# First batch of a spectral filter: the order in which a second transpose writes, and one 128-column matmul per point of the last transform

## The chip, the cores and the metric

The kernel runs on one core of a Trainium2 chip. The metric is the device time of one launch in microseconds; a time quoted for the kernel is the median of several runs. One further execution was recorded by the hardware profiler. Its engines are called PE (TensorE), PEld (the weight loads of TensorE), DVE (VectorE), ACT (ScalarE), POOL (GpSimd) and SP (SyncE, which issues DMAs). All times below are microseconds unless ns is written.

## What is computed

```python
def _attn_ref(x, filt_r, filt_i):                 # x: 8 x 3008 x 256
    X = np.fft.rfft(x, axis=1)
    F = (filt_r + 1j * filt_i)[None, :, :]
    y = np.fft.irfft(X * F, n=x.shape[1], axis=1)
    return y.astype(np.float32)

def _moe_ref(x, w_in, w_out):                     # 24064 tokens, 256 -> 2048 -> 256
    h = x @ w_in
    g = np.maximum(0.01 * h, h)
    return g @ w_out

reference(...) = _moe_ref(_attn_ref(x, filt_r, filt_i).reshape(24064, 256), moe_w_in, moe_w_out)
```

Each of 8 batches is filtered along its 3008 positions in the frequency domain; then every token goes through two matrix products with a leaky ReLU between them.

## The kernel before

**Transforms as matmuls.** 3008 is 94 x 32, written n = 32 n1 + n2. The filter is done in four matmul steps. Step 1 transforms over n1 with the constant `fwd1`. Step 2 transforms over the 32 values of n2 (with the twiddle factors in the constant `f2_sb`), and the result is multiplied by the filter. Step 3, called `sa` in the names, transforms back to n2 (`inv2r`, `inv2i`). Step 4, called `sb`, transforms back to n1 (constant `i1_sb`, one 128 x 94 matrix for each n2) and gives `yt`, the filtered batch with the feature d on the partitions: `yt[:, dt]` holds the features of half dt, 128 partitions by 3008 positions. Between steps 1 and 2, and between 3 and 4, the data has to be turned. In batches 1 to 7 that goes through a scratch array in DRAM. In the first batch, where nothing else can run yet, VectorE turns it with a 32 x 32 block transpose of 4-byte words; each word is a pair of neighbouring 2-byte values (d even, d odd).

**The first batch by hand.** `FIRST` (L461) is a list of steps in the order in which they are issued; each engine takes its own steps in that order. `sap` (L417) is step 3 for four values; `sae` (L422) evacuates it from PSUM to `big[2]`. The helper `paired` (L278) views a tile as (e n t): for each e (one of 64 word columns in a half) and each of 32 n, two neighbouring values t. `t2 i` (L426) transposes a quarter of `big[2]` into `big[0]`, 128 x 1024 words; quarters 0 and 1 belong to half dt = 0, quarters 2 and 3 to dt = 1. `sbp dt h b` (L440) does step 4 for half dt and the four n2 of group h, into the PSUM bank b; the data of `big[0]` is the stationary operand (the weights) and `i1_sb[:, n2, :]` is streamed. `sbe` (L443) evacuates the 128 x 376 result into `yt`, on ScalarE (A) or VectorE (D), through `quad_copy` (L333). In the list stand all eight groups of dt = 0 and the groups 0 and 1 of dt = 1. The transposes are issued in the order 1, 0, 3, 2, after VectorE's last multiplies by the filter (`s2d`, L402).

**The rest is planned.** After the list, the MoE runs over 47 chunks of 512 tokens, 8 planner time units a chunk (`SL`). All later work is a heap of (time, function) pairs; what has the earliest planned time is issued first. The first MoE product (`moe1`, L499) needs `yt` for both halves; L509 is its matmul, L514 its evacuation with the leaky ReLU. The second product is L634 in the first three chunks and L573 later. The transforms of the next batches (L254, L303, L325, L346) are planned between these matmuls. The groups 2 to 7 of step 4 for dt = 1 of the first batch are planned there too: `late_sb` (L446), six calls at the times in `REST`, among the first nine chunks' matmuls. They call the same `sb_matmuls` (L431) as `sbp`. Step 4 of the later batches is `sb_group` (L338): one matmul (L346) for each n2 with 128 columns of weights and 96 rows.

**Layout of `big[0]` before.** Written by `t2` as (h n e r): for each half h, each pair of n2 (n), each of 64 e, the two n2 of the pair (r) side by side. One partition's word for e and n2 has, as its neighbour, the word for the same e and the other n2 of the pair. Since a word holds two values t, `sb_matmuls` reads, for one n2, the values of one t at every fourth 2-byte place: 64 columns for t = 0 and 64 for t = 1, in two matmuls that write the PSUM partitions 0 to 63 and 64 to 127. `sae` puts the features 0 to 63 of a half into t = 0 and 64 to 127 into t = 1, so that the two results are in the order of d.

Of the kernel before, what the change touches and what calls it, by code (L numbers as in the profile page):

```python
# [13 lines left out]
FP32 = mybir.dt.float32  # L14
# [7 lines left out]
Q = 32  # L22
# [53 lines left out]
def kernel(  # L76
# [9 lines left out]
    nc = tc.nc  # L86
# [42 lines left out]
    i1_sb = cpool.tile([P, N2, N1], FP16, name="i1_sb")  # L129
# [7 lines left out]
    big = [cpool.tile([P, Q * D], FP16, name=f"big{i}") for i in range(3)]  # L137
# [140 lines left out]
    def paired(t):  # L278
        return t[:].rearrange("p (e n t) -> p n e t", n=Q, t=2)
# [79 lines left out]
    held, spare = {}, [scrp.tile([P, 4, DH], FP32, tag=f"p{i // 2 + 1}", name=f"spare{i}") for i in range(6)]  # L359
# [61 lines left out]

    def sae(hf, c, e):  # L422
        engine[e](paired(big[2])[:, ds(c, 4), ts(hf, DH // 2)],
                  held.pop(("sa", hf, c)).rearrange("p n (t e) -> p n e t", t=2))

    def t2(i):  # L426
        a = big[2][:].bitcast(FP32)[:, ts(i, E4 * Q)].rearrange("p (e n r) -> p e n r", n=Q // 2, r=2)
        o = big[0][:].bitcast(FP32).rearrange("p (h n e r) -> p h e n r", h=2, n=Q // 2, r=2)
        nc.vector.transpose(o[:, i // 2, ts(i % 2, E4)], a)

    def sb_matmuls(ps, dt, h):  # L431
        assert ("i1t",) not in issued
        src = big[0][:].rearrange("p (h n e r t) -> p h n r t e", h=2, n=Q // 2, r=2, t=2)
        for j in range(4):
            n2 = 4 * h + j
            for t in range(2):
                nc.tensor.matmul(ps[64 * t : 64 * t + 64, j, :], src[:, dt, n2 // 2, n2 % 2, t, :],  # L437
                                 i1_sb[:, n2, :], start=True, stop=True)

    def sbp(dt, h, b):  # L440
        sb_matmuls(fill(("sb", dt, h), b, 4, N1), dt, h)
# [4 lines left out]
    def late_sb(dt, h, copy):  # L446
        ps = bank("pf", 4, N1)
        sb_matmuls(ps, dt, h)
        quad_copy(h, dt, ps, copy)
# [8 lines left out]
    def round_x(n0, n, e):  # L458
# [19 lines left out]
        sbe 0 3 D, sbe 1 0 D  # L478
    """
    steps = dict(s1p=s1p, s1e=s1e, t1=t1, s2p=s2p, s2d=s2d, s2a=s2a, s2m=s2m, sap=sap, sae=sae, t2=t2,  # L480
                 sbp=sbp, sbe=sbe, x=load_x, w_out=load_w_out, xc=round_x, warm=keep_warm)
    for step in FIRST.split(","):
# [190 lines left out]
    for b in range(1, B):  # L673
        z = 47 * (b - 4) if b > 4 else 0
        p = PLANS[min(b, 4) - 1]
# [18 lines left out]
    while queue:  # L694
        time, n, stage, b, g, f = heapq.heappop(queue)
        t = max(time, last + GAP)
# [61 lines left out]
```

## Time and profile before

| what | value |
|---|---|
| median of 3 runs | 748.44 (747.7 to 749.98) |
| span of the profiled execution, first to last instruction | 747.3 |
| L437, the matmuls of step 4 in the first batch | 128, median 238 ns each in the record |
| L437, weight loads (128 x 64) | 128, median 158 ns |
| L346, the same step in the later batches | median 206 ns; weight loads (96 x 128) 98 ns |
| L423, evacuation of step 3, 128 x 512 | 10 of median 619 ns and 2 of 646 ns |
| L429, the second transpose | 4 of median 1220 ns, from 28.9 to 33.6 |
| L437, first and last start | 31.3 and 80.3 |

A row of the engine part of the profile gives busy time, share of the span and number of instructions. Matmuls are pipelined: the length in the record is the time of one from its start to its end, and the next one starts long before that, so the rate is read from the distance of starts. The chain of waits is followed backwards from the last instruction, at each step to the instruction that released it. A timeline row gives start, length, engine, line, operation, what is written and read, and how many of them were merged; in brackets the idle time of the engine before it and what ended it.

### The profile page before, as it was taken

Reading aid. Unit: us, or ns where it says so; the run is one execution under the profiler, and the core shown is the slowest. Engines: PE = TensorE matmul, PEld = TensorE weight load, DVE = VectorE, ACT = ScalarE, POOL = GpSimd, SP = SyncE. Lnnn points to the kernel's source line nnn. Section 1 sums busy time; section 2 is a strip of 40 time slices with the busy share of each in tenths; the row PEclk is TensorE's granted clock in tenths of the full one; section 3 lists DMA queues with packets and bytes.
Section 4 is the critical chain, followed back from the end, with each engine's and each line's share of the span. In section 5 each row is a group of like instructions: output and inputs, shape, how many; then the busy total and the mean of one; then the engine's idle time right before and its main releaser. Section 6 shows DMA issues by size and latency. Waiting matters only on the chain.

```text
span 747.3 us, 19408 instructions
## 1 busy us (share of the span) xinstructions
PE 738.1 (99%) x8017; PEld 528.8 (71%) x8017; DVE 504.8 (68%) x684; ACT 559.2 (75%) x755; POOL 165.0 (22%) x171
## 2 busy tenths in 40 slices
PE   8999999999999999999999999999999999999997
PEld 3556667776777777877778777777777777777776
DVE  5887647866686776766776667766676676465565
ACT  4776797888878787777777787787777777777662
POOL 6503421332322213131232222121212210000000
PEclk9999999999999999999999999999999999999999
DMA  9997797887876667665676656543454333111012
GB/s 206 228 223 190 188 229 218 196 207 200 209 185 154 151 182 188 158 144 163 189 185 150 159 157 172 158 137 111 143 165 116 101 103 111 51 54 54 29 49 67
DMA packets 119560, 113.64 MB, mean 152 GB/s; under 512 B 16352, under 2 KB 92768, under 8 KB 119280
## 3 DMA queue, kind: packets, MB, share of 16 engines
q1 hardware_dynamic: 104128, 94.66, 43.1%
q0 software_dynamic: 15056, 17.49, 16.1%
q8 instruction: 62, 1.02, 0.6%
q10 hardware_dynamic: 288, 0.26, 0.1%
q14 instruction: 26, 0.21, 0.1%
HBM read 57.51 MB, written 50.33 MB: 144 GB/s over the span
## 4 chain that ended last, share of the span: by engine, by line
PE 92%; DMA 4%; DVE 2%; POOL 0%; ACT 0%; issue 0%; SPq 0%; POOLq 0%; DVEq 0%
PE ph L509 42%; PE po_ps L573 18%; PE pf L573 18%; PE pf L254 3%; PE pf L346 3%; PE pf L303 2%; PE pf L325 2%; DMA p_b_g<-p_b_g 2%; PE pf L634 1%; PE po_ps L634 1%; DMA f_sb<-fwd_const 1%; DMA x_sb<-in_x_dram 1%; DVE big L546 0%; POOL y_b_g L318 0%; ACT yt L336 0%; PE pf L437 0%
## 5 line engine op out<-in xcount | busy, mean ns | idle before, releaser
L514 ACT ACTIVATE gt_c<-ph 128x1024 f16<-128x1024 f32 x376 | 385.6, 1026 | 134.5 <-PE ph L509 123.8
L509 PE MATMUL ph<-yt,w_in_sb 128*128 128x512 f16 (+7 forms) x1728 | 447.3, 351 | 0.2 <-ACT yt L336 0.2
L573 PEld LDWEIGHTS <-gt_c 128*128 128x128 f16 x2800 | 202.2, 98 | 91.3 <-issue 0.2
L318 POOL TENSOR_TENSOR y_b_g<-p_b_g,p_b_g 128x512 f16<-128x512 f32 x84 | 115.1, 1372 | 417.8 <-DMA p_b_g<-p_b_g 295.8
L573 PEld LDWEIGHTS <-big 128*128 128x128 f16 x2128 | 151.3, 98 | 61.6 <-issue 0.2
L509 PEld LDWEIGHTS <-w_in_sb 128*128 128x128 f16 x1728 | 137.5, 98 | 19.7 <-DVE yt L336 0.4
L312 DVE TENSOR_TENSOR p_b_g<-pf,fb_sb 128x512 f32<-128x512 f32 x78 | 53.7, 688 | 31.9 <-PE pf L303 19.0
L573 PE MATMUL po_ps<-wt_sb,gt_c 128*128 128x128 f16 x704 | 70.0, 219 | 0.0
L573 PE MATMUL pf<-wt_sb,gt_c 128*128 128x128 f16 x688 | 68.4, 219 | 0.1
L573 PE MATMUL pf<-w_out_sb,gt_c 128*128 128x128 f16 x720 | 67.9, 219 | 0.0
L573 PE MATMUL po_ps<-wt_sb,big 128*128 128x128 f16 x720 | 67.4, 219 | 0.0
L573 PE MATMUL pf<-wt_sb,big 128*128 128x128 f16 x704 | 67.2, 219 | 0.0
L573 PE MATMUL po_ps<-w_out_sb,gt_c 128*128 128x128 f16 x688 | 66.0, 219 | 0.0
L257 ACT CAST big<-pf 128x512 f16<-128x512 f32 x98 | 57.1, 588 | 11.9 <-PE pf L254 10.5
L336 ACT CAST yt<-pf 128x376 f16<-128x376 f32 x120 | 56.3, 472 | 10.7 <-PE pf L346 7.7
L546 DVE TENSOR_TENSOR big<-gt_c 128x2048 f16<-128x2048 f16 (+1 forms) x46 | 59.1, 1284 | 0.1
L315 DVE TENSOR_TENSOR p_b_g<-pf,fa_sb 128x512 f32<-128x512 f32 x84 | 57.2, 681 | 0.2
L546 DVE TENSOR_TENSOR gt_c<-gt_c 128x2048 f16<-128x2048 f16 x43 | 56.1, 1306 | 1.0
L546 DVE TENSOR_TENSOR big<-gt_c,big 128x2048 f16<-128x2048 f16 (+1 forms) x45 | 56.3, 1251 | 0.0
L546 DVE TENSOR_TENSOR big<-big,gt_c 128x2048 f16<-128x2048 f16 (+1 forms) x45 | 55.6, 1235 | 0.1
L327 ACT CAST big<-pf 128x512 f16<-128x512 f32 x84 | 49.0, 584 | 4.9 <-PE pf L325 3.0
L254 PE MATMUL pf<-x_sb,small_sb 94*128 94x512 f16 x109 | 41.6, 381 | 0.0
(91 smaller groups left out, 622.9 us busy)
## 6 DMA issues: line engine op xcount, KB each, us to landing
dz<-big SPq DMA_DIRECT2D x98, 256.0 KB
p_b_g<-p_b_g SPq DMA_DIRECT2D x156, 128.0 KB
out_dram<-ost_c_h SPq DMA_DIRECT2D x118, 128.0 KB
big<-dz SPq DMA_DIRECT2D x42, 256.0 KB
big<-dz SPq DMA_DIRECT2D x56, 192.0 KB
x_sb<-in_x_dram POOLq DMA_DIRECT2D x40, 192.0 KB, 4.6
x_sb<-in_x_dram POOLq DMA_DIRECT2D x2, 768.0 KB, 8.9
w_in_sb<-in_moe_w_in_dram POOLq DMA_DIRECT2D x1, 1024.0 KB, 13.2
```

What stands on the lines that cost most here:

```text
L254: nc.tensor.matmul(ps, fwd1[:N1], x_sb[:N1, ds(2 * g, 2), :], start=True, stop=True)
L257: copy(st[:, ds(2 * (g % 2), 2), :], ps)
L312: nc.vector.tensor_tensor(p2[:], ps, fb, AL.mult)
L315: nc.vector.tensor_tensor(p1[:], ps, fa, AL.mult)
L318: ("y", b, g), lambda: nc.gpsimd.tensor_tensor(y1[:], p1[:], p3[:], AL.add)))
L327: nc.scalar.copy(st2[h % 4][:, ds(2 * (g % 2), 2), :], ps)
L336: copy(yv, ps.rearrange("p c a -> p a c"))
L346: nc.tensor.matmul(ps[:, j, :], z2[h % 4][:K4, j, ts(dt, P)], i1_sb[:K4, 4 * h + j, :], start=True, stop=True)
L509: nc.tensor.matmul(ph[:, j, ds(t - ci * CH, e - t)], w_in_sb[:, dt, ts(ct, P)], yt[:, dt, ds(t % N, e - t)], start=(dt == 0), stop=(dt == ...
L514: nc.scalar.activation(gts[ci][:, ds(2 * g, 2), :], ph, AF.Lrelu)
L546: nc.vector.tensor_tensor(*(v[:, ds(c0, n)] for v in (o, i0, i1)), op)
L573: nc.tensor.matmul(po[:, t], a()[:, c, ts(t, P)], w[:, c, :], start=(c == 0), stop=(c == NCH - 1))
```

## The change

Three helpers of the first batch change; the list of steps, the planner and all instructions' places in their engines' orders stay.

```diff
     def sae(hf, c, e):
         engine[e](paired(big[2])[:, ds(c, 4), ts(hf, DH // 2)],
-                  held.pop(("sa", hf, c)).rearrange("p n (t e) -> p n e t", t=2))
+                  held.pop(("sa", hf, c)).rearrange("p n (e t) -> p n e t", t=2))
 
     def t2(i):
         a = big[2][:].bitcast(FP32)[:, ts(i, E4 * Q)].rearrange("p (e n r) -> p e n r", n=Q // 2, r=2)
-        o = big[0][:].bitcast(FP32).rearrange("p (h n e r) -> p h e n r", h=2, n=Q // 2, r=2)
+        o = big[0][:].bitcast(FP32).rearrange("p (h n r e) -> p h e n r", h=2, n=Q // 2, r=2)
         nc.vector.transpose(o[:, i // 2, ts(i % 2, E4)], a)
 
     def sb_matmuls(ps, dt, h):
         assert ("i1t",) not in issued
-        src = big[0][:].rearrange("p (h n e r t) -> p h n r t e", h=2, n=Q // 2, r=2, t=2)
+        src = big[0][:].rearrange("p (h n d) -> p h n d", h=2, n=Q)
         for j in range(4):
             n2 = 4 * h + j
-            for t in range(2):
-                nc.tensor.matmul(ps[64 * t : 64 * t + 64, j, :], src[:, dt, n2 // 2, n2 % 2, t, :],
-                                 i1_sb[:, n2, :], start=True, stop=True)
+            nc.tensor.matmul(ps[:, j, :], src[:, dt, n2], i1_sb[:, n2, :], start=True, stop=True)
```

The evacuation puts d = 2e + t into the word e, so that the two values of a word are neighbours in d. The transpose writes, for each n2, the 64 words of e one behind the other, which are then 128 values in the order of d. Its writes come in the same order as before (e, then the 32 n2), but consecutive words now lie 64 words apart, where before two lay side by side and the next two 128 words on. The last transform takes 128 consecutive columns as weights, in one matmul for each n2: 64 matmuls of 128 x 94 in place of 128 of 64 x 94, with as many weight loads.

## The prediction

> **What bounds the kernel now.** I read the engine totals and the summary of the chain of waits first.
>
> ```profile
> PE 738.1 (99%) x8017; PEld 528.8 (71%) x8017; DVE 504.8 (68%) x684; ACT 559.2 (75%) x755; POOL 165.0 (22%) x171
> ...
> PE 92%; DMA 4%; DVE 2%; POOL 0%; ACT 0%; issue 0%; SPq 0%; POOLq 0%; DVEq 0%
> ```
>
> TensorE (PE) is busy for 99% of the span and carries 92% of the chain that ended last, so a saved PE slot in the long stream is a saved slot of the whole. The exception is the head, before the MoE's stream begins; there the chain, in order of time (start, length, engine, tile, line), runs over other engines:
>
> ```profile
> 27.80 1.22 DVE prod L400
> 29.02 2.29 DVE big L429 x2
> ...
> 31.35 0.47 PE pf L437 x6
> ...
> 31.84 2.74 ACT yt L336 x7
> ...
> 34.62 1.18 PE ph L509 x4
> ```
>
> The second transpose (L429, two of its four pieces) holds PE until 31.35; seven ScalarE evacuations (L336) then hold the first MoE matmul until 34.62. The VectorE timeline shows all four transposes in one unbroken run that ends at 28.93 + 4.71 = 33.64:
>
> ```profile
> 28.93 4.71 DVE L429 STREAM_TRANSPOSE big<-big 128x1024 f32<-128x1024 f32 x4
> ```
>
> So two nearly equal strands end at the same place: ScalarE's evacuations, and transposes, then the dt = 1 matmuls of L437 (from 33.70), then the last evacuations (ScalarE 34.43 + 0.52 = 34.95). The second L509 matmul needs the latter and starts at 35.00.
>
> **Part 1: six late groups of the last transform (L446).** They lie in PE's full stream. The PE timeline around one:
>
> ```profile
> 40.94 0.59 PE L509 MATMUL ph<-yt,w_in_sb 128*128 128x512 f16 x2
> 41.46 0.45 PE L437 MATMUL pf<-i_sb,big 128*64 128x94 f16 x8
> 41.84 0.39 PE L254 MATMUL pf<-x_sb,small_sb 94*128 94x512 f16 x1
> 42.07 1.03 PE L509 MATMUL ph<-yt,w_in_sb 128*128 128x512 f16 x4
> 42.93 0.38 PE L254 MATMUL pf<-x_sb,small_sb 94*128 94x512 f16 x1
> ```
>
> Lengths of one matmul overlap the next, so I count from start to start. Four L509 take 42.93 - 42.07 = 0.86, or 0.216 each. The two at 40.94 are therefore issued by 41.37, and the group's slot is 41.84 - 41.37 = 0.47, with about 0.09 lost before its first and 0.13 after its last matmul (beyond 4 pairs of 0.061). L254 then takes 0.23 to the next start, 0.01 over its 0.22. What replaces it stands in the same trace: later batches do this transform with four 94-column matmuls on full-width weights.
>
> ```profile
> 109.94 0.22 PE L573 MATMUL po_ps<-wt_sb,gt_c 128*128 128x128 f16 x1
> 109.99 0.34 PE L346 MATMUL pf<-i_sb,big 96*128 96x94 f16 x4
> 110.17 0.39 PE L573 MATMUL po_ps<-wt_sb,gt_c 128*128 128x128 f16 x4
> ```
>
> That slot is 0.18 (0.045 a matmul), with no loss on either side. The saving is 0.47 + 0.01 - 0.18 = 0.30 a group, 6 x 0.305 = **1.83 us**. The rows differ in contraction (96 rows against 128); if the new matmuls came at L573's 0.055 the saving would be 1.6.
>
> **Part 2: the ten groups of the head (L441).** From 0.245 a group to 0.18. PE has slack between them, so only the first and the last count: the first evacuation starts about 0.1 earlier, and the two dt = 1 groups end about 0.12 earlier (eight matmuls at 0.045 against eight pairs at 0.061). Gain 0.12 at L509.
>
> **Part 3: the evacuations of L423.** They read d in order instead of two strands 64 apart, and write the same 4-byte pairs. With L283, which already has the new form, ScalarE takes 0.607 and 0.637 for this size against medians of 0.619 and 0.646: 0.01 x 12 less. Not on the path: VectorE reaches the transposes from its own multiplies (L400). I take nothing. Its last one ends at 30.58 + 0.66 = 31.24, 0.03 before the third transpose, so cover is thin, but the sign is a gain.
>
> **Part 4: the transposes of L429.** Same four instructions, same reads. The written order changes: before, two 4-byte words lie side by side (8 bytes) and the next pair is 512 bytes on; after, each 4-byte word is 256 bytes from the next. No row here writes single words so. The nearest (line, engine, operation, count, then minimum, median and maximum in ns):
>
> ```profile
> L429 DVE STREAM_TRANSPOSE big<-big x4: 1204/1220/1247, 28.9 to 32.4; 128x1024 f32<-128x1024 f32 x4
> ...
> L283 DVE CAST big<-pf x4: 682/688/693, 8.5 to 13.4; 128x512 f16<-128x512 f32 x4
> ...
> L283 DVE CAST big<-ph x2: 1225/1226/1226, 10.3 to 11.6; 128x1024 f16<-128x1024 f32 x2
> ...
> L336 DVE CAST yt<-pf x4: 511/546/550, 33.6 to 73.9; 128x376 f16<-128x376 f32 x4
> ```
>
> Lower end: the cost goes by element. L336 reads 376 single words 376 bytes apart from PSUM in 0.546, 1.05 ns each after a fixed 0.15; then 1,024 words cost what they cost now, +0. (I exclude a gain: 1,024 x 1.05 + 0.15 = 1.22 is today's time.) Upper end: it goes by separate piece. L283 writes 4-byte pieces 128 bytes apart; 512 against 256 pieces differ by 1.226 - 0.688 = 0.538, so 2.1 ns a piece; L429's 512 pieces of 8 bytes fit the same price. With 1,024 pieces a transpose takes 0.15 + 1,024 x 2.1 = 2.30, **+1.08 each**. ScalarE's L283 writes lie between: 1.028 against 0.607 for 256 pieces more, 1.64 ns a piece, 1.83 a transpose, +0.61. I take the upper end: L283 is the nearest row, the same engine writing the same 4-byte pieces into the same memory, while the lower end rests on a read of another memory. That is a choice: every row fits both prices, because each writes two elements a piece.
>
> [...]
>
> At +1.08: PE's first L437 goes from 31.35 to 33.51; the last transpose ends at 33.64 + 4.33 = 37.97. Behind it on VectorE stand only the two evacuations at 33.57 and 34.25. PE restarts at 38.03, the eight dt = 1 matmuls are done at 38.59, ScalarE's last evacuation ends at 39.10 (0.47, undisturbed), and the second L509 starts at 39.15 instead of 35.00: +4.15, with part 2 in it. ScalarE's seven others move by 2.16 only and cease to matter. SP's and POOL's later issues move with PE; no DMA is added or passed.
>
> **Sum.** +4.15 - 1.83 = +2.3 on the span of 747.3, or 749.6; the median of the runs, 748.44, stands 1.1 above that span, which I keep: **750.7 us**. In the stream nothing else fills the gap that PE gains: the one place where VectorE holds PE (L303 at 66.04) hangs on VectorE waits that PE ended at 57.79 and 59.66, so it moves along.
>
> **The rivals.** *A, the writes go by element (other side):* -0.12 - 1.83 = -1.95, **746.5**. For: L336's single-word reads at full rate. Against: that is PSUM, and read. It decides below +0.49 a transpose, where 4 x 0.49 = 1.95. *A2, the VectorE stretch before 66.04 doesn't move and takes back four groups' saving (4 x 0.305 = 1.22):* **747.7**. For: the chain goes through it; against: the two waits named. *B, ScalarE's price, +0.61:* 2.45 - 1.95 = +0.5, **748.9**. *C, the clock drops in the new PE gaps* (30.97 to 33.51, and some 2.5 us before 38.03). Against it the clock after PE's last matmul (issued by 742.4), here by stretch (its length, the busy time of PE, PE's weight loads, VectorE, ScalarE and GpSimd, the granted clock, the DMA share and GB/s):
>
> ```profile
> 744.20:746.00 1.80, 0.00 (x0) 0.00 (x0) 0.00 (x0) 0.00 (x0) 0.00 (x0) 1.00 0.47 144
> 746.00:747.20 1.20, 0.00 (x0) 0.00 (x0) 0.00 (x0) 0.00 (x0) 0.00 (x0) 0.54 0.00 0
> ```
>
> It holds through 3.6 us without PE, longer than either gap. If it fell all the same: at the start idle-tile matmuls come 0.43 apart from 1.20 to 5.43 instead of 0.216, so some 4.2 us at half speed, 2.1 lost: **752.8**. *D, the full-width loads don't run at 0.045 beside this data:* bounded in part 1 by 0.2.
>
> **How the numbers follow.** Forecast 0.47, A 0.28, A2 0.05, B 0.13, C 0.07. A measurement of this kernel can tell about 0.3%, 2.25 us, from no change: the bounds are 746.2 and 750.7. The forecast lies on the upper one; what I left out there (evacuations bunched behind the last transpose, PE's restart) adds time, so I give two thirds of it to slower, 0.32, and with C 0.39. A lies 0.3 from the lower bound: 0.18 faster, 0.10 same; add 0.02 of doubt in part 1's slot. Faster 0.20, same 0.41, slower 0.39. The forecast's own range is 750.0 to 751.6; with A and part of C it must reach from 745.9 to 752.3, which leaves out the low tail of A (0.08) and most of C (0.06).
>
> **What would show it.** L429's time: 2.3 is the forecast, 1.2 is A, 1.8 is B. Start of the second L509: 39.1, 34.9, 37.3. The slots of the six late groups 0.18; the wait before L303 near 66 unchanged; granted clock 1.00 from 31 to 45. The forecast is wrong if L429 stays under 1.7.

## The result and the profile after

| | before | changed |
|---|---|---|
| median | 748.43 us (6 runs) | 751.56 us (6 runs) |
| ratio of the times, 95% interval | | 1.0037 [1.0028, 1.0047] |
| span of the profiled execution | 747.3 | 749.6 |
| mean granted clock in it | 0.999 | 0.996 |

The change made the kernel slower, by 3.1 us by the medians and by 2.8 by the ratio. Line numbers after it are two lower behind the edit: L507 is L509 of before, L512 is L514, L436 the former L437. The page of the changed kernel, engine totals and chain of waits:

```profile
PE 737.7 (98%) x7953; PEld 528.0 (70%) x7953; DVE 502.9 (67%) x684; ACT 559.1 (75%) x755; POOL 165.0 (22%) x171
...
PE 93%; DVE 3%; DMA 2%; ACT 1%; issue 1%; POOL 0%; SPq 0%; DVEq 0%; POOLq 0%; ACTq 0%
```

PE lost the 64 matmuls, and the head's VectorE part of the chain grew. The chain in order of time (start, length, what):

```profile
28.59 7.22 DVE big L429 x4
...
35.86 0.35 PE ph L436 x4
...
36.42 0.48 ACT yt L336
...
36.94 1.42 PE ph L507 x3
38.36 0.43 PE pf L254
38.78 0.85 PE ph L507 x2
```

Now all four transposes stand in the chain, not two, and ScalarE's seven evacuations have left it. Two things are to be seen. The run of transposes took 7.29 us instead of 4.71 (28.51 to 35.80), so that the second first-product matmul started at 36.94 instead of 35.00, although the transposes had started 0.42 earlier (in the chain of the kernel before, a load of `f_sb` that landed at 19.15 stands ahead of them; in this one no load does). And the matmuls that follow are twice as far apart as before: three L507 take 1.42, where four L509 took 1.18, and two take 0.85 instead of 0.43. The transposes' own row (minimum, median, maximum in ns) of the changed kernel:

```profile
L429 DVE STREAM_TRANSPOSE big<-big x4: 1878/1920/2000, 28.5 to 33.9; 128x1024 f32<-128x1024 f32 x4
```

The same kernel by stretches of 3.41 us, the length of the fall in the granted clock (length, busy time of PE, its weight loads, VectorE, ScalarE, GpSimd, then granted clock, DMA share, GB/s):

```profile
33.58:36.99 3.41, 1.47 (x19) 0.91 (x18) 3.14 (x4) 2.35 (x6) 0.00 (x0) 1.00 1.12 189
37.00:40.41 3.41, 3.41 (x9) 1.23 (x10) 0.93 (x2) 1.02 (x1) 0.05 (x1) 0.50 1.46 199
40.41:43.82 3.41, 3.41 (x17) 1.48 (x16) 3.20 (x5) 3.05 (x4) 1.36 (x2) 1.00 0.83 106
```

PE was busy for 1.47 us of the first 3.41 (modelled ends included), and for the next 3.41 us its clock was half: 9 matmuls, against 17 in the stretch after it. A late group in the PE timeline:

```profile
44.55 0.59 PE L507 MATMUL ph<-yt,w_in_sb 128*128 128x512 f16 x2
44.99 0.34 PE L436 MATMUL pf<-i_sb,big 128*128 128x94 f16 x4
45.16 0.38 PE L254 MATMUL pf<-x_sb,small_sb 94*128 94x512 f16 x1
```

From 44.55 + 2 x 0.216 = 44.98 to 45.16: the slot is 0.18, where it was 0.47. The other five groups, counted the same way, go from 0.47 or 0.48 to 0.18 as well.

As a ledger, the same instruction's start in both traces (after minus before): the second first-product matmul +1.94; the third evacuation of the first product, behind the slow clock (42.17 against 38.56), +3.61; the 25th, behind the six late groups (84.92 against 82.79), +2.14; the last one +2.31. The late groups gave back 1.47 net.

### The profile page after: what moved, and what is told of

It is laid out like the page before. It is cut to its first block, busy times and chain, and to the rows that moved or that the text cites. A ratio compares the mean times of both kernels' runs of the same rounds, so it can differ in the third digit from the quotient of the medians.

```text
span 749.6 us, 19280 instructions
## 1 busy us (share of the span) xinstructions
PE 737.7 (98%) x7953; PEld 528.0 (70%) x7953; DVE 502.9 (67%) x684; ACT 559.1 (75%) x755; POOL 165.0 (22%) x171
## 4 chain that ended last, share of the span: by engine, by line
PE 93%; DVE 3%; DMA 2%; ACT 1%; issue 1%; POOL 0%; SPq 0%; DVEq 0%; POOLq 0%; ACTq 0%
PE ph L507 42%; PE po_ps L571 18%; PE pf L571 18%; PE pf L254 3%; PE pf L346 3%; PE pf L325 2%; PE pf L303 2%; PE po_ps L368 1%; PE po_ps L632 1%; PE pf L632 1%; DVE big L429 1%; DMA p_b_g<-p_b_g 1%; DMA dz<-big 1%; DMA big<-dz 0%; PE ph L396 0%
## 5 line engine op out<-in xcount | busy, mean ns | idle before, releaser
L512 ACT ACTIVATE gt_c<-ph 128x1024 f16<-128x1024 f32 x376 | 385.2, 1025 | 134.8 <-PE ph L507 124.1
L507 PE MATMUL ph<-yt,w_in_sb 128*128 128x512 f16 (+7 forms) x1728 | 448.6, 352 | 0.5 <-ACT yt L336 0.3
L507 PEld LDWEIGHTS <-w_in_sb 128*128 128x128 f16 x1728 | 137.7, 98 | 20.8 <-issue 2.0
L336 ACT CAST yt<-pf 128x376 f16<-128x376 f32 x120 | 56.4, 472 | 13.3 <-PE pf L346 8.1
L544 DVE TENSOR_TENSOR big<-gt_c 128x2048 f16<-128x2048 f16 (+1 forms) x46 | 56.4, 1226 | 0.1
L544 DVE TENSOR_TENSOR gt_c<-gt_c 128x2048 f16<-128x2048 f16 x43 | 54.4, 1266 | 1.0
```

The costliest lines, as they stand in the source:

```text
L336: copy(yv, ps.rearrange("p c a -> p a c"))
L507: nc.tensor.matmul(ph[:, j, ds(t - ci * CH, e - t)], w_in_sb[:, dt, ts(ct, P)], yt[:, dt, ds(t % N, e - t)], start=(dt == 0), stop=(dt == ...
L512: nc.scalar.activation(gts[ci][:, ds(2 * g, 2), :], ph, AF.Lrelu)
L544: nc.vector.tensor_tensor(*(v[:, ds(c0, n)] for v in (o, i0, i1)), op)
```

## The experiments

Each median is set against the kernel before, measured beside it on the same chip: 748.85 in a first series of four experiments, 749.13 in a second.

**The order of the writes alone.**

```diff
-        o = big[0][:].bitcast(FP32).rearrange("p (h n e r) -> p h e n r", h=2, n=Q // 2, r=2)
+        o = big[0][:].bitcast(FP32).rearrange("p (h n r e) -> p h e n r", h=2, n=Q // 2, r=2)
...
-        src = big[0][:].rearrange("p (h n e r t) -> p h n r t e", h=2, n=Q // 2, r=2, t=2)
+        src = big[0][:].rearrange("p (h n r e t) -> p h n r t e", h=2, n=Q // 2, r=2, t=2)
```

> The evacuation and the two 64-column matmuls of before, with the transpose writing in the new order (part 4 of the prediction alone). Theory: the four transposes take 1.9 us each (they start 1.78 apart instead of 1.17), PE stands idle before the first and before the last groups, and the clock falls to half for 3.4 us afterwards as in the changed kernel; nothing is saved in the late groups. So +1.9 at the head with the 0.1 of part 2 not gained, +1.7 from the clock: about +3.8 us against before. Rival 1 (the time lies in the matmuls on contiguous columns and not in the transposes): L429 at 1.2 us and within 0.5 us of before. Rival 2 (the clock's fall belongs to the changed matmuls): +2.0 us and a clock that stays at 1.00.

Measured: 751.63 against 748.85, ratio 1.0031 [1.0018, 1.0044], or +2.3 us by the ratio (+2.8 by the medians). The transposes, and the two stretches around the idle time:

```profile
L429 DVE STREAM_TRANSPOSE big<-big x4: 1901/1953/2001, 28.8 to 34.2; 128x1024 f32<-128x1024 f32 x4
```

```profile
32.55:35.96 3.41, 2.03 (x64) 1.64 (x64) 3.41 (x3) 2.73 (x7) 0.00 (x0) 1.00 0.98 195
35.96:39.38 3.42, 2.95 (x27) 1.50 (x28) 2.07 (x5) 1.50 (x2) 0.11 (x1) 1.00 1.42 198
```

The write order by itself makes the transposes dear and the kernel slower, so rival 1 falls. The clock didn't fall in this profile, although PE stands idle here too, for 1.53 us before its restart at 36.19; what differs from the changed kernel is the 64 half-width matmuls between the pauses, and what that may mean comes with the filled stretches below. My +3.8 was too high by that, and by a thing I hadn't seen: the weight columns now lie 4 bytes apart instead of 8, and the late groups got cheaper too:

```profile
43.23 0.60 PE L509 MATMUL ph<-yt,w_in_sb 128*128 128x512 f16 x2
43.75 0.36 PE L437 MATMUL pf<-i_sb,big 128*64 128x94 f16 x8
44.05 0.39 PE L254 MATMUL pf<-x_sb,small_sb 94*128 94x512 f16 x1
```

The slot is 44.05 - 43.66 = 0.39, against 0.47, and the other five groups are cheaper by 0.08 as well. For this execution the parts add up: the second first-product matmul starts at 37.29, 2.29 later than before; less 6 x 0.08 that is +1.8, and the span is 1.7 longer (749.0 against 747.3). So here rival 2 is right. For the other executions the mean granted clock is on record. It is 0.997 in the two slowest (753.27 and 753.48), lower than in any execution of the kernel before, so the clock probably fell there too; the remaining seven, at 0.998 and 0.999, can't be told from the kernel before by it. How much of the median's excess is such falls isn't shown.

**The matmuls alone.** The sb_matmuls of the change with the transpose and the evacuation of before.

```diff
-        src = big[0][:].rearrange("p (h n e r t) -> p h n r t e", h=2, n=Q // 2, r=2, t=2)
+        src = big[0][:].rearrange("p (h n d) -> p h n d", h=2, n=Q)
...
-            for t in range(2):
-                nc.tensor.matmul(ps[64 * t : 64 * t + 64, j, :], src[:, dt, n2 // 2, n2 % 2, t, :],
-                                 i1_sb[:, n2, :], start=True, stop=True)
+            nc.tensor.matmul(ps[:, j, :], src[:, dt, n2], i1_sb[:, n2, :], start=True, stop=True)
```

> The transpose of before, with one 128x128 matmul on the 128 columns as they lie (parts 1 and 2 alone); the features of the first batch are therefore mixed up and its output is not the reference's. Theory: the late groups' slots fall from 0.47 to 0.18 us, L429 stays at 1.2, the clock stays at 1.00, the head gains 0.1: -1.9 us against before. Rival (the saving in the late groups is taken back where VectorE holds PE near 66 us): -0.7 us.

Measured: 747.45 against 748.85, ratio 0.9979 [0.9968, 0.9991], -1.6 us by the ratio (-1.4 by the medians). A late group:

```profile
40.04 0.59 PE L507 MATMUL ph<-yt,w_in_sb 128*128 128x512 f16 x2
40.48 0.34 PE L436 MATMUL pf<-i_sb,big 128*128 128x94 f16 x4
40.65 0.38 PE L254 MATMUL pf<-x_sb,small_sb 94*128 94x512 f16 x1
```

The slot is 0.18. The interval holds the -1.9 expected and ends where the rival's -0.7 lies; the rival is the less likely of the two, and the copies below bear on it again.

**The idle stretches filled.**

```diff
-        ... sae 1 0 A, warm 4, sbp 0 1 b1, ... sbp 0 5 b3, sbp 1 0 b4, ...
+        ... sae 1 0 A, warm 11, sbp 0 1 b1, ... sbp 0 5 b3, warm 7, sbp 1 0 b4, ...
```

> The changed kernel with seven more idle-tile matmuls before the first group of the last transform and seven before its first dt = 1 group, where PE stands idle for 1.8 and 1.7 us. Theory: the clock no longer falls, so the first MoE matmuls run at full rate: 1.7 us less than the changed kernel, about +0.6 us against before. Rival (the idle time itself, or a late start of something else, holds the head, and the lower clock is hidden): the same time as the changed kernel, +2.3 to +3 against before.

Measured: 749.97 against 748.85, ratio 1.0012 [1.0000, 1.0023], or +0.9 us by the ratio; the interval holds the theory's +0.6 and not the rival's +2.3. Since the changed kernel had run elsewhere, both were run once more side by side.

> The changed kernel once more, beside the next one on the same chip. Theory: the clock falls to half for 3.4 us after PE's two idle stretches in all or most executions, since little of PE's work lies in the 3.4 us before 37: +3 us against before, 1.7 more than the next kernel. Rival (the fall is a matter of luck in one profile): less than 1 us more than the next kernel.

> The changed kernel with seven more idle-tile matmuls in each of the two idle stretches once more, beside the changed kernel on the same chip. Theory: +0.6 to +1.2 us against before with a clock of 1.00 through the head, 1.7 less than the changed kernel; what is left is 4 x 0.61 of the transposes less 1.8 of the late groups. Rival: no difference from the changed kernel.

Measured: changed 751.47, ratio 1.0036 [1.0023, 1.0048]; filled 749.63, ratio 1.0010 [1.0001, 1.0019]; before 749.13. The fill is worth 1.84 us by the medians, where 1.7 was expected. The changed kernel's second profile, by stretches:

```profile
32.44:35.85 3.41, 1.80 (x34) 1.44 (x31) 3.41 (x3) 2.70 (x7) 0.00 (x0) 1.00 1.04 203
35.86:39.26 3.40, 3.27 (x13) 1.15 (x11) 1.16 (x3) 1.50 (x2) 0.00 (x0) 0.50 1.43 197
```

and the filled one's, followed by its chain:

```profile
34.06:37.47 3.41, 2.97 (x26) 1.36 (x23) 2.96 (x4) 2.12 (x6) 0.00 (x0) 1.00 1.16 188
37.47:40.89 3.42, 3.42 (x17) 1.53 (x16) 2.51 (x4) 2.53 (x4) 0.90 (x2) 1.00 1.52 194
```

```profile
28.80 7.31 DVE big L429 x4
...
37.23 0.81 PE ph L507 x3
```

The clock fell in both profiles of the changed kernel and in neither of the filled one. Nor is it luck of two profiles: the mean granted clock of each execution is on record, and a fall to half for 3.41 us takes 1.7 / 750 = 0.0023 from it. All nine executions of the changed kernel in this series show 0.994 to 0.996 (three of them 0.994, lower than one such fall and the one after PE's last matmul explain), and so do five of the six behind the first result; the sixth shows 0.998. The 21 of the filled kernel and the 56 of the kernel before lie between 0.998 and 1.000. The three L507 take 0.81 instead of 1.42, although the transposes are as dear as in the changed kernel (7.31). The idle time itself stays: the second first-product matmul starts at 37.23, no earlier.

What the fall depends on is less clear. In every profile the granted clock changes only at whole multiples of 3.41 us after its first rise (37.00 - 6.28 = 30.72 = 9 x 3.413 in the changed kernel's first profile), so the stretches lie on a fixed grid. The stretches before the two falls weren't without work: PE was busy for 1.47 and 1.80 us in them. But PE's busy time doesn't decide it either. After these two stretches of the same grid, one in the changed kernel just before its low one, the other at the end of the kernel with the new order alone, the clock held:

```profile
30.17:33.58 3.41, 1.78 (x27) 1.19 (x26) 3.41 (x3) 1.51 (x5) 0.00 (x0) 1.00 1.05 219
...
742.53:745.94 3.41, 1.47 (x27) 1.30 (x24) 1.26 (x3) 0.00 (x0) 0.00 (x0) 1.00 0.23 79
```

With 1.47 us of busy time it fell in one kernel and held in another. The columns streamed by the matmuls that start in a stretch do put the stretches in order. It fell after 16 x 94 + 2 x 512 = 2,528 columns (33.58) and 29 x 94 = 2,726 (32.44); it held after 24 x 94 + 512 = 2,768 (30.17), 23 x 128 = 2,944 (742.53), and 64 x 94 = 6,016 (32.55, the order alone; 3,008 if a half-width matmul counts half). Over all ten profiles the nine falls inside the span came after at most 2,726 columns, and no stretch at full clock with 2,768 or more was followed by one. That is a count over traces in which some matmul records may be missing, with an edge that rests on two stretches; no run set the columns on purpose. By it, one whole matmul in place of two halves, which streams half as many columns, has a share in the fall beside the pauses.

**What a scattered write costs.** Behind the last work of the kernel before, each on 1,024 words (the changed kernel's transposes, with single words 256 bytes apart, took 1.92), for instance:

```diff
+    nc.vector.transpose(words[:, :2048].rearrange("p (n r e) -> p e n r", n=16, r=2)[:, 0:32], given)
+    nc.vector.transpose(words.rearrange("p (e n r u) -> p u e n r", n=16, r=2, u=4)[:, 0], given)
+    copy(words[:, :2048].rearrange("p (n e) -> p e n", n=32)[:, 0:32], flat)
```

> The kernel before with eleven VectorE and ScalarE instructions on 1,024 words behind its last work, which write nothing that is used: transposes that write contiguous words, pairs 256 bytes apart, single words 256, 16 and 8 bytes apart, then copies on VectorE and on ScalarE: contiguous, writing single words 256 bytes apart, reading single words 256 bytes apart. [...] Rival 1 (any write that isn't to the next word is slow): 8 bytes apart 1.9 as well. Rival 2 (it is a matter of the transpose): the copies that write scattered words take what the contiguous ones take. The kernel's time is before's plus some 17 us.

Measured in one execution, VectorE's timeline, in the order of the expectation (the pairs lie 512 bytes apart, as in the kernel before):

```profile
742.70 1.24 DVE L731 STREAM_TRANSPOSE big<-fb_sb 128x1024 f32<-128x1024 f32 x1
743.97 1.25 DVE L732 STREAM_TRANSPOSE big<-fb_sb 128x1024 f32<-128x1024 f32 x1
745.25 1.90 DVE L733 STREAM_TRANSPOSE big<-fb_sb 128x1024 f32<-128x1024 f32 x1
747.19 1.98 DVE L734 STREAM_TRANSPOSE big<-fb_sb 128x1024 f32<-128x1024 f32 x1
749.20 1.25 DVE L735 STREAM_TRANSPOSE big<-fb_sb 128x1024 f32<-128x1024 f32 x1
750.48 0.69 DVE L738 COPY big<-fb_sb 128x1024 f32<-128x1024 f32 x1
751.21 1.03 DVE L739 COPY big<-fb_sb 128x1024 f32<-128x1024 f32 x1
752.28 1.03 DVE L740 COPY big<-fb_sb 128x1024 f32<-128x1024 f32 x1
```

and ScalarE's copies, contiguous, scattered write, scattered read:

```profile
753.34 1.04 ACT L738 COPY big<-fb_sb 128x1024 f32<-128x1024 f32 x1 [16.17 <-DVE big L740]
754.41 1.92 ACT L739 COPY big<-fb_sb 128x1024 f32<-128x1024 f32 x1
756.37 1.92 ACT L740 COPY big<-fb_sb 128x1024 f32<-128x1024 f32 x1
```

Single words 256 bytes apart cost a transpose 1.90, 16 bytes apart 1.98, but 8 bytes apart 1.25, no more than side by side. So rival 1 falls, and the step lies between 8 and 16 bytes. Why it lies there isn't shown. It costs 0.65 to 0.74 us on 1,024 words, not the forecast's 1.08. Rival 2 is half right. ScalarE pays for a scattered copy (1.92 against 1.04), reading as well as writing. VectorE's copy writes scattered words in 1.03, about 1 ns each, a rate that its transpose doesn't reach in the same order; against its contiguous copy (0.69) it still loses 0.34. Why the two operations of one engine differ wasn't tried. The kernel took 761.13, 12.3 more than before and not 17: the added work begins beside the last 5 us of the kernel, in which VectorE has next to nothing to do.

**The change for one half only.** New order, whole matmuls and the new evacuation for dt = 1, to which the six late groups belong; dt = 0 as before.

```diff
...
+        of = "p (h n r e) -> p h e n r" if i > 1 else "p (h n e r) -> p h e n r"
+        o = big[0][:].bitcast(FP32).rearrange(of, h=2, n=Q // 2, r=2)
...
+            if dt:
+                nc.tensor.matmul(ps[:, j, :], whole[:, dt, n2], i1_sb[:, n2, :], start=True, stop=True)
+                continue
...
-        ... sbp 0 5 b3, sbp 1 0 b4, ...
+        ... sbp 0 5 b3, warm 5, sbp 1 0 b4, ...
```

> The change for dt = 1 alone (the half that the six late groups belong to), dt = 0 as before, and five more idle-tile matmuls before the first dt = 1 group. Theory (a transpose in the new order costs 0.6 us more, a late group saves 0.3, the clock falls only when PE stands idle): two dear transposes instead of four, L429 at 1.2, 1.2, 1.9, 1.9 us, the second first-product matmul about 1.0 us later than before, six slots of 0.18: +1.0 - 1.8 = -0.8 us against before, clock 1.00. Rival (the head's delay comes from more than the transposes' own time): no better than the changed kernel with the gaps filled, +0.6 to +1.1.

Measured: 748.67 against 749.13, ratio 0.9994 [0.9986, 1.0003]. The chain:

```profile
28.82 6.05 DVE big L430 x4
...
36.00 0.81 PE ph L514 x3
```

Two dear transposes make the run 6.05 in the chain (6.12 in the timeline), between 4.71 and 7.3, and the second first-product matmul comes at 36.00, 1.0 later than before, as expected. The middle of the interval, -0.4, is half of the -0.8 expected; the interval holds both -0.8 and no change, and excludes the rival's +0.6.

**The late groups from a copy.** The head as before; GpSimd puts each late group's data in the order of d shortly before it is used.

```diff
...
+    def late_copy(dt, h):
+        src = big[0][:].rearrange("p (h n e r t) -> p h n r t e", h=2, n=Q // 2, r=2, t=2)
+        in_order[dt, h] = y = ypp.tile([P, 4, DH], FP16, tag="y", name=f"late{h}")
+        to = y[:].rearrange("p (n r) (t e) -> p n r t e", r=2, t=2)
+        for i in range(2):
+            nc.gpsimd.tensor_copy(to[:, i], src[:, dt, 2 * h + i])
...
+            nc.tensor.matmul(ps[:, j, :], y[:, j, :], i1_sb[:, 4 * h + j, :], start=True, stop=True)
...
+        at(REST[g - 10] - 1.5, lambda g=g: late_copy(1, g - 8))
```

> Everything of before in the head (old order, two 64-column matmuls), but each of the six late groups is first put in the order of d by two GpSimd copies into a tile of the y pool, and then takes four 128-column matmuls. Theory: the six slots fall to 0.18 us, no transpose gets dearer, PE never stands idle for long: -1.8 us against before, the best of all kernels here. Rival 1 (GpSimd's copies come late or hold up its y additions, and PE waits for them): a gap before L303 or the late groups, and no gain. Rival 2 (the saved slots are taken back near 66 us, where VectorE holds PE): -0.6 us.

Measured: 747.41 against 749.13, ratio 0.9982 [0.9974, 0.9991]: -1.3 us by the ratio (-1.7 by the medians), faster than both kernels. A late group, and two of GpSimd's steps:

```profile
41.53 0.60 PE L520 MATMUL ph<-yt,w_in_sb 128*128 128x512 f16 x2
41.97 0.34 PE L459 MATMUL pf<-i_sb,late 128*128 128x94 f16 x4
42.14 0.38 PE L254 MATMUL pf<-x_sb,small_sb 94*128 94x512 f16 x1
```

```profile
35.71 0.76 POOL L453 COPY late<-big 128x256 f16<-128x256 f16 x2
...
38.09 0.76 POOL L453 COPY late<-big 128x256 f16<-128x256 f16 x2
```

The slot is 0.18 again, and 0.76 us of copies a group lie on an engine that had the time. The interval, -1.9 to -0.7, holds the six slots' 1.83 and leaves out rival 2's -0.6, narrowly. Rival 1 foresaw a gap and no gain. There is a gap in this profile, 0.50 us before L303 at 60.00, where PE waits for a DMA; but the half kernel, which has no copies, has it too (0.81 at 60.71), and the gain came all the same.

## Why the prediction held, and where it didn't

The time came out 0.9 above the forecast and inside its own range, but by two errors of opposite sign and almost equal size. The sum isn't evidence for its terms.

- **Part 1** (late groups, -1.83): right. The slot was 0.18 in the changed kernel and in three experiments, and the gain reached the end of the kernel: -1.3 to -1.7 with the copies, -1.4 to -1.6 with the matmuls alone.
- **Part 2** (head, -0.12): right in kind. The first evacuation starts 0.39 after the first matmul of step 4 instead of 0.49, and the second first-product matmul starts 1.14 after the last transpose instead of 1.36.
- **Part 3** (evacuations, a gain of 0.01 each that I took as nothing): the gain isn't there, 0.622 and 0.692 by the medians against 0.619 and 0.646. The two longer ones run beside the new transposes and take 0.698 in the kernel with the new order alone, where the evacuation is that of before. They aren't on the path: the last one ends at 30.83, the third transpose starts at 32.14.
- **Part 4** (transposes, +1.08 each): the direction was right, the price wrong in kind and in size. A transpose took 1.92, +0.70 in length and +0.65 in the run of four (7.29 - 4.71 = 2.58 in all). I took VectorE's price for a separate 4-byte piece, 2.1 ns, from the nearest row. By it, 1,024 single words 8 bytes apart would have cost 2.30 too, and they took 1.25: a separate piece isn't dear as such, but single words 16 and 256 bytes apart were (1.98 and 1.90 in the probe). The row that I took follows as well from 1.05 ns an element at two elements a piece. And it isn't so that every row fitted both prices: `quad_copy` writes its 376 values side by side, so that a price by written pieces gives L336 nothing, while it took 0.546. ScalarE's 1.64 ns, which I put down as rival B, gave 1.83, and was nearest. The delay of PE was +2.36, counted from the start of the transposes, not +4.15.
- **Rival C** (the clock, chance 0.07): I argued it away, and it happened, in both profiles of the changed kernel and by the mean clock in 14 of 15 executions. The evidence was the clock that held for 3.6 us after PE's last matmul, which I read as a rule on the longest pause. On the grid, that matmul lies in a stretch (739.28 to 742.69) in which PE was busy for 3.01; the first stretch without any work ends at 746.11, and there the clock fell. So the hold says nothing of shorter pauses. Here two of 1.63 and 1.52 us in the record, with 32 matmuls of 94 columns between them, went ahead of a fall. The price that I gave, 2.1, was 1.67 in the ledger and 1.84 by the pair of runs.
- **A2** (VectorE holds PE near 66 us): rightly set aside; the gap before L303 moved along, to 68.79, with 1.05 us in the record instead of 0.95.

What happened is thus B and C together, which as the prediction priced them come to 748.9 + 2.1 = 751.0; it had weighed each by itself, at 0.13 and 0.07.

With the measured terms: +2.36 - 0.42 (the execution's earlier start) + 1.67 - 1.83 = +1.8, against a span longer by 2.3; the rest is in waits of 0.1 to 0.4 that differ from one profile to the next, such as 0.27 for a DMA before L346 at 112.56.

## What to carry to other kernels

Writing words one by one can cost an engine that is not the bottleneck more than the bottleneck saves, if the writer stands alone in the head of the kernel (here 2.58 us in four transposes, 256 bytes from word to word, against 1.83 in six late groups); where rows fit two prices, a probe of a few instructions decides what a choice of row can't. When a step makes TensorE wait, add up the columns that it streams in each 3.4 us around the wait rather than looking for one long pause alone (in these traces the columns, 2,726 and fewer against 2,768 and more, and not the longest pause, told the falls from the holds), and fill the pause with idle matmuls (worth 1.84 us here). A better layout for late consumers can be made later, by an engine with time to spare, instead of in the step that everything waits for.

## What was not expected of the hardware

- VectorE's 32 x 32 transpose took 1.90 us for 1,024 single words 256 bytes apart and 1.98 for 16 bytes, against 1.24 to 1.25 side by side, in pairs or 8 bytes apart, while its copy writes or reads single words 256 bytes apart in 1.03 (0.69 side by side). ScalarE's copy took 1.92 for them on either side, against 1.04.
- PE's clock fell to half for 3.41 us after stretches of 3.41 us in which PE was busy for 1.47 and, in another execution, 1.80; it held after others with 1.47 and 1.78. By streamed columns the falls lie at 2,726 and fewer, the holds at 2,768 and more.
- Eight matmuls on 64 weight columns took a slot of 0.47 us with the columns 8 bytes apart and 0.39 with 4 bytes.
